# Another order of small products, block products and state steps in the repeated unit of a recurrent-attention and MLP kernel

## The chip, the cores and the metric

The kernel runs on one core of a Trainium2 chip. The metric is device time in microseconds (us) of one execution; times of several executions are given by their median. A profiled execution has a trace besides: a span from its first to its last instruction, and a start and a duration for every instruction.

## The reference

The kernel computes a gated recurrence over 768 steps for 4 batches of 8 heads with 48 channels, and then a normalized MLP on the 384 channels that the heads make together:

```python
for t in range(S):
    state = f[:, :, t, :, None] * state + einsum('bhd,bhde->bhde', k[:, :, t], v[:, :, t])
    y[:, :, t] = einsum('bhd,bhde->bhe', q[:, :, t], state)
x  = y as (B, S, 384)
xn = (x - mean) / sqrt(var + 1e-06) * g_ln
out = x + relu(xn @ w_ch1) @ w_ch2          # w_ch1 384 x 1536, w_ch2 1536 x 384
```

(f is a sigmoid of an input; the einsum of k and v is an outer product. All of it is in float32.)

## The kernel before, in words

**Chunks.** The 768 steps are cut into 12 chunks of 64 steps. A chunk of all four batches has 256 tokens, which lie as two groups of 128 rows. The attention of a chunk and its MLP are written as small stages, and the stages of several chunks run beside each other.

**The order of the work is written by hand.** Two strings of tokens, `START` and `UNIT`, are read by `run` (at the end of the kernel), and each token issues the instructions of one stage. Every engine works off its own instructions in that order, and a wait of one instruction holds all that stand behind it on the same engine. DMAs issued by SP stand in one line too. `START` covers the first chunks. `UNIT` is then run for m = 3 to 11: token `m{m}` is the next step of the MLP of chunk m, `a{n}.x` is stage x of the attention of chunk n = m+1, `a{o}.x` of chunk m+2. `l`/`L` load raw inputs, `p`/`P` split one half of a raw input into two 16-bit planes (a copy on ACT, L439) and send it to DRAM (L440, by POOL for `p`, by SP for `P`), `x` turns it on its way back (a transposing DMA of SP, L454), `s` makes sums for the second MLP layer, `y` sums for the first.

**The attention stages that matter here:**
- `gates` (ACT, L695), `after` and `upto` (DVE scans, L668, L680), `q` (L725 and L728) and `k` (L716) make the scaled q and k, `kept` (L738) the decayed state of the chunk before.
- `carried` (TensorE, L757): 32 small matmuls of the kept state with q. `scores` (L771): 32 small matmuls of k with q. `causal` (DVE, L777) masks them.
- `kt`: a transposing DMA of SP (L454) brings the scaled k back turned. `values` (L807): 32 small matmuls of masked scores with v, and three copies of the result to x on ACT (L816, L818). `chunk` (L845): 32 small matmuls of turned k with v, for chunks up to 10 only. `state` (DVE, L853) adds them to the kept state.
- `stats` (DVE, L830, L831, and two small instructions on POOL, L833, L834), `norm` (DVE, L875) and `turn` (six TensorE transposes, L886, and six ACT copies into `xt`, L888) prepare the MLP.

A small matmul uses a 64 x 64 part of the array, and four parts work side by side; all other matmuls use the array of 128 x 128.

**The MLP of a chunk has 22 steps.** The first layer (`by_blocks`, from L936) is a fast block product: fifteen products of four 128x128x128 matmuls each (L951), whose results stand in PSUM banks with the names bw, bx, by, bv and bz. Behind each product either ACT copies the bank into the block of h that it belongs to (L956), or DVE adds it to the block (L959, L997), and ACT applies the ReLU (L962). `bx` and `by` are used again and again: a product into a bank can only start when the bank's last result has been read. The sums `y` (DVE, L921) are inputs of these products. The second layer is seven products of six matmuls each (L1045), in the order p1, p2, p6, p5, p7, p3, p4; the sums `s` (DVE, L930 to L933) are inputs of p6, p5 and p3. Their results are gathered by DVE (L1053) and POOL (L1053 too): p1x, then p1 += p6, u2x = p1 + x (POOL), p1 += p5, u4x and u4y (POOL), and then u2x, u4y and u4x take p7, p3 and p4 and go out by SP.

**PSUM banks.** Four one-bank tiles go round (`one_bank`, `bufs=4`): the five names of the first layer, the seven products of the second layer and the two transposes of `turn` take them in turn, so each product of the second layer waits until an older result in its bank has been read. The small matmuls have banks of their own; `scores` and `chunk` share one (`shared`).

Of the kernel before, what the change touches and what calls it, by code (L numbers as in the profile page):

```python
# [14 lines left out]
ALU = mybir.AluOpType  # L15
# [300 lines left out]
U m2 m1 p4K0 a5.gates  # L316
"""
UNIT = """
a{o}.after m{m} m{m} a{n}.carried p{o}q1 a{n}.scores a{n}.causal m{m} P{o}q0 m{m} m{m} m{m}
m{m} a{n}.values m{m} p{p}f1 a{o}.upto a{n}.kt m{m} m{m} a{n}.stats m{m} m{m} l{p}k p{p}f0 m{m}  # L320
a{n}.chunk m{m} a{n}.norm m{m} x{o}k x{o}q P{p}k0 m{m} s{m} a{n}.turn a{n}.state l{p}v p{p}k1
m{m} m{m} a{o}.q m{m} a{o}.k L{z}f y{n} p{o}K0 x{p}f l{p}q p{o}K1 m{m} m{m} m{m} a{o}.kept
a{p}.gates
"""


# [1 line left out]
def kernel(  # L328
# [21 lines left out]
    P = 128  # L350
# [585 lines left out]
    def by_blocks(n, h):  # L936


        a, y = y_of.pop(n)
        v, b = late["v"], late["b"]  # L940
        KB = CW // P
        out = {(g, j): h[:, (j - 1) * KB:j * KB, (g - 1) * P:g * P] for g in (1, 2)
               for j in (1, 2, 3)}
        banks = {}

        def product(bank, left, right):
            new = bank not in banks
            if new:
                banks[bank] = one_bank(f"{bank}_{n}").rearrange("p (i t) -> p i t", t=P)
            for i in range(KB):  # L950
                nc.tensor.matmul(banks[bank][:, i], lhsT=right[:, i * P:(i + 1) * P], rhs=left,  # L951
                                 start=new and i == 0, stop=True, skip_group_check=True)
            return banks[bank]

        def copy(to, bank, scale=1.0):
            nc.scalar.activation(out=out[to], in_=bank, func=AF.Copy, scale=scale)  # L956

        def add(to, bank, op=ALU.add):
            nc.vector.tensor_tensor(out=out[to], in0=out[to], in1=bank, op=op)  # L959

        def relu(to, bank=None):
            nc.scalar.activation(out=out[to], in_=out[to] if bank is None else bank, func=AF.Relu)  # L962

        copy((1, 3), product("bw", y[12], b[2, 3]))
        yield
        copy((2, 3), product("bx", y[11], v[11]))
        yield
        copy((1, 1), product("bv", y[3], b[2, 1]))
        yield
        add((1, 3), product("bx", y[9], b[3, 3]))  # L970
        yield
        add((1, 1), product("by", y[4], b[1, 1]))
        yield
        add((1, 1), product("bx", a[1, 3], v[7]), ALU.subtract)
        relu((1, 1))
        yield
        add((1, 3), product("by", a[1, 1], v[13]), ALU.subtract)
        relu((1, 3))
        yield
        copy((1, 2), product("bx", y[10], v[10]))  # L980
        yield
        add((1, 2), product("by", y[1], v[1]), ALU.subtract)
        yield
        copy((2, 2), product("bz", a[2, 2], v[0]), -1.0)
        yield
        add((2, 2), product("bx", y[2], b[3, 2]), ALU.subtract)
        yield
        add((2, 2), product("by", y[14], b[1, 2]))
        relu((2, 2))
        yield  # L990
        add((1, 2), product("bz", y[6], b[2, 2]))
        relu((1, 2))
        yield
        relu((2, 1), product("bx", y[8], v[8]))
        yield
        bank = product("by", y[5], v[5])
        nc.vector.tensor_tensor(out=out[2, 3], in0=bank, in1=out[2, 3], op=ALU.subtract)  # L997
        relu((2, 3))
        yield

    def mlp(n):
# [134 lines left out]
    for m in range(3, NU):  # L1136
# [4 lines left out]
        if m == NU - 2:  # L1141
# [5 lines left out]
                                    op=ALU.min)  # L1147
# [39 lines left out]
```

## Time and profile before

| | |
|---|---|
| median of 3 runs | 437.86 us (437.38 to 440.23) |
| profiled execution | 437.34 us, its span 435.6 us, the rest outside the span 1.7 us |
| granted TensorE clock, mean | 0.985 |
| one repeated unit, from p1 of chunk 6 to p1 of chunk 7 (258.23 to 290.72) and on to p1 of chunk 8 (323.20) | 32.49 and 32.48 us |
| the same from chunk 3 to chunk 4 (160.33 to 193.27) | 32.94 us |
| last matmul ends | 429.2 us |

In the timeline, a row has start, duration, engine, line, operation, output<-inputs, shapes and count; rows of equal instructions that follow each other are merged, and square brackets hold how long the engine had sat idle and what ended that. A matmul in float32 is recorded as two instructions, so a product of four matmuls is x8, a group of 32 small ones x64. PE is TensorE, PEld its weight loads, which run ahead of the matmuls.

### The profile page before, as it was taken

The numbers are of one execution on the slowest core, as the hardware profiler recorded it, in microseconds if no ns is written. First come the engines' busy times: TensorE is split into PE (matmuls) and PEld (weight loads), VectorE is DVE, ScalarE is ACT, GpSimd is POOL, SyncE is SP. The second block draws the span as 40 slices with busy tenths as digits, with TensorE's granted clock in tenths as the row PEclk, the third lists the DMA queues.
The fourth block names the chain that finished last, engine by engine and source line by source line (L and its number), as shares of the span: only waits on it lengthen the run. The fifth ranks groups of instructions, "written<-read, shape, count | busy, mean of one in ns | idle before, by whom it ended". The sixth has DMA issues, their size and how long they took to land.

```text
span 435.6 us, 12925 instructions
## 1 busy us (share of the span) xinstructions
PE 418.5 (96%) x5429; PEld 389.0 (89%) x5429; DVE 338.3 (78%) x539; ACT 214.7 (49%) x364; POOL 125.8 (29%) x148
## 2 busy tenths in 40 slices
PE   5599999999999999999999999999999999999994
PEld 4589987668979999999999999999999999999993
DVE  5998798745986779779779779779779879475451
ACT  2484857443534573574474574574574552350320
POOL 2362453560033026016026016025025015021030
PEclk9699999999999999999999999999999999999998
DMA  9999979887977899699599799699698751401001
GB/s 171 286 212 192 236 227 222 204 198 184 180 154 148 181 208 228 187 200 212 155 211 204 169 187 212 180 188 218 165 196 198 136 117 47 91 2 23 15 9 34
DMA packets 167647, 71.68 MB, mean 165 GB/s; under 512 B 151760, under 2 KB 157840, under 8 KB 167584
## 3 DMA queue, kind: packets, MB, share of 16 engines
q1 hardware_dynamic: 151728, 54.38, 62.9%
q0 software_dynamic: 3872, 12.64, 8.6%
q10 hardware_dynamic: 11984, 3.79, 4.1%
q8 instruction: 44, 0.72, 0.7%
q14 instruction: 19, 0.16, 0.1%
HBM read 28.31 MB, written 23.59 MB: 119 GB/s over the span
## 4 chain that ended last, share of the span: by engine, by line
PE 89%; DVE 3%; ACT 2%; SPq 1%; issue 1%; POOL 1%; DMA 1%; ACTq 0%; DVEq 0%; POOLq 0%
PE pp L1045 31%; PE bx L951 12%; PE by L951 9%; PE ph L1016 7%; PE po L1026 5%; PE bz L951 4%; PE ph L900 3%; PE py L807 3%; PE shared L771 3%; PE py L757 2%; PE bv L951 2%; PE bw L951 2%; PE shared L845 2%; PE xp L886 2%; SPq L474 1%
## 5 line engine op out<-in xcount | busy, mean ns | idle before, releaser
L962 ACT ACTIVATE h<-h 128x512 f32<-128x512 f32 x45 | 28.3, 631 | 49.4 <-DVE h L959 42.0
L1045 PE MATMUL pp<-mixed,h 128*128 128x192 f32 x240 | 42.3, 326 | 0.0
L1045 PE MATMUL pp<-w,h 128*128 128x192 f32 x240 | 42.1, 326 | 0.0
L1045 PE MATMUL pp<-mixed,s 128*128 128x192 f32 x240 | 40.9, 326 | 0.2 <-DVE p1x L1053 0.2
L1045 PEld LDWEIGHTS pp<-mixed,s 128*128 128x128 f32 x240 | 39.2, 190 | 0.5 <-DVE p1x L1053 0.5
L1045 PEld LDWEIGHTS pp<-mixed,h 128*128 128x128 f32 x240 | 39.5, 190 | 0.1
L439 ACT COPY Kplanes<-kh 128x1024 uint16<-128x1024 uint16 x18 | 18.2, 1047 | 42.9 <-DVE kh L716 15.0
L1045 PEld LDWEIGHTS pp<-w,h 128*128 128x128 f32 x240 | 38.7, 190 | 0.3
L668 DVE TENSOR_TENSOR_SCAN after<-gates,ends 128x1040 f32<-128x1040 f32 (+1 forms) x13 | 29.8, 2291 | 6.7 <-ACT gates L699 3.4
L1026 PE MATMUL po<-w,h 128*128 128x384 f32 x96 | 32.3, 489 | 0.0
L1016 PE MATMUL ph<-xt,w 128*128 128x256 f32 x144 | 31.9, 380 | 0.2 <-ACT xt L888 0.2
L959 DVE TENSOR_TENSOR h<-h,by 128x512 f32<-128x512 f32 x36 | 24.8, 688 | 8.6 <-PE by L951 5.0
L1016 PEld LDWEIGHTS ph<-xt,w 128*128 128x128 f32 x144 | 27.1, 190 | 4.3 <-ACT xt L888 0.5
L951 PE MATMUL bx<-y,v 128*128 128x128 f32 x216 | 30.2, 283 | 0.0
L959 DVE TENSOR_TENSOR h<-h,bx 128x512 f32<-128x512 f32 x27 | 18.4, 683 | 13.8 <-PE bx L951 13.8
L680 DVE TENSOR_TENSOR_SCAN upto<-gates,starts 128x1040 f32<-128x1040 f32 (+1 forms) x13 | 28.1, 2158 | 0.5
L1026 PEld LDWEIGHTS po<-w,h 128*128 128x128 f32 x96 | 17.8, 190 | 11.3
L440 POOL DMA_DIRECT2D fhalves<-fplanes x14 | 8.4, 597 | 66.8 <-ACT fplanes L439 66.8
L951 PEld LDWEIGHTS bx<-y,v 128*128 128x128 f32 x216 | 26.2, 191 | 0.9
L1053 POOL TENSOR_TENSOR p1x<-p,x 128x192 f32<-128x192 f32 x10 | 11.6, 1163 | 47.1 <-ACT p L1060 47.1
L562 POOL TENSOR_TENSOR w<-w_0upper,w_0units 128x768 int32<-128x768 int32 x7 | 14.6, 2084 | 28.7 <-DVE w_0upper L560 16.5
L888 ACT ACTIVATE xt<-xp,gain 128x128 f32<-128x128 f32 x72 | 20.0, 380 | 5.4 <-PE xp L886 5.4
(171 smaller groups left out, 961.3 us busy)
## 6 DMA issues: line engine op xcount, KB each, us to landing
w_0words<-in_moe_w_ch_dram SPq DMA_DIRECT2D x7, 768.0 KB, 5.8
v<-in_v_dram SPq DMA_DIRECT2D x46, 96.0 KB, 4.0
Khalves<-Kplanes POOLq DMA_DIRECT2D x16, 256.0 KB, 3.8
kraw<-in_k_dram SPq DMA_DIRECT2D x40, 96.0 KB, 4.4
fhalves<-fplanes POOLq DMA_DIRECT2D x14, 256.0 KB, 4.7
kraw<-in_q_dram SPq DMA_DIRECT2D x36, 96.0 KB, 3.6
fraw<-in_f_logit_dram ACTq DMA_DIRECT2D x27, 96.0 KB, 3.7
khalves<-kplanes POOLq DMA_DIRECT2D x9, 256.0 KB, 3.9
```

The lines of the kernel that those rows point to most:

```text
L439: nc.scalar.copy(out=to, in_=src)
L562: nc.gpsimd.tensor_tensor(out=to.bitcast(I32), in0=upper, in1=units, op=ALU.add)
L668: nc.vector.tensor_tensor_scan(out=at["after"].rearrange(flat)[:, c0:c1][:, ::-1], data0=gt[:, c0 + 1:c1 + 1][:, ::-1], data1=ends.rearran ...
L680: nc.vector.tensor_tensor_scan(out=at["upto"].rearrange(flat)[:, c0:c1], data0=gt[:, c0:c1], data1=starts.rearrange(flat)[:, c0:c1], initi ...
L771: nc.tensor.matmul(ps[half(b), r, e], lhsT=kh[head_rows(r), seg], rhs=qh[head_rows(r), seg], start=True, stop=True)
L888: nc.scalar.mul(out=xt[:, m, g * P:(g + 1) * P], in_=pt[:, m], mul=gain[:, m:m + 1])
L951: nc.tensor.matmul(banks[bank][:, i], lhsT=right[:, i * P:(i + 1) * P], rhs=left, start=new and i == 0, stop=True, skip_group_check=True)
L959: nc.vector.tensor_tensor(out=out[to], in0=out[to], in1=bank, op=op)
L962: nc.scalar.activation(out=out[to], in_=out[to] if bank is None else bank, func=AF.Relu)
L1016: nc.tensor.matmul(ph[:, j], lhsT=w1[:, m, (i + j) * P:(i + j + 1) * P], rhs=xt[:, m], start=m == 0, stop=m == KD - 1)
L1026: nc.tensor.matmul(po, lhsT=h[:, i, g * P:(g + 1) * P], rhs=w2[:, i], start=i == 0, stop=i == KF - 1)
L1045: nc.tensor.matmul(pp, lhsT=a[:, i], rhs=b[:, i], start=i == 0, stop=i == KH - 1)
```

## The change

It does three things, all in the repeated unit; `START` stays as it is.

1. The token string `UNIT` is written anew. `carried` and `scores` stand at the start of the unit, ahead of the first block product. `values` and `chunk` stand next to each other, ahead of the last two block products. `kt` is the first token. `turn` stands between the last two products of the second layer, `stats` behind `chunk`, `norm` and `state` later than before, and the loads and splits are spread otherwise.
2. `by_blocks` runs its fifteen products in another order and with other banks for some.
3. Two helpers, `copied` and `added`, do a product and its reading in one call; the instructions are the same, but for two: block (1, 2) now begins with the copy of one product with scale -1, and the other product is added.

```diff
 UNIT = """
-a{o}.after m{m} m{m} a{n}.carried p{o}q1 a{n}.scores a{n}.causal m{m} P{o}q0 m{m} m{m} m{m}
-m{m} a{n}.values m{m} p{p}f1 a{o}.upto a{n}.kt m{m} m{m} a{n}.stats m{m} m{m} l{p}k p{p}f0 m{m}
-a{n}.chunk m{m} a{n}.norm m{m} x{o}k x{o}q P{p}k0 m{m} s{m} a{n}.turn a{n}.state l{p}v p{p}k1
-m{m} m{m} a{o}.q m{m} a{o}.k L{z}f y{n} p{o}K0 x{p}f l{p}q p{o}K1 m{m} m{m} m{m} a{o}.kept
-a{p}.gates
+a{n}.kt a{n}.carried p{p}f1 a{o}.after a{n}.scores m{m} a{n}.causal m{m} m{m} m{m} P{o}q0 m{m}
+m{m} m{m} m{m} m{m} a{o}.upto m{m} p{o}q1 p{p}f0 m{m} m{m} m{m} x{o}k a{n}.values l{p}k
+a{n}.chunk m{m} a{n}.stats m{m} x{o}q s{m} p{p}k1 P{p}k0 L{z}f a{o}.q a{o}.k m{m} x{p}f m{m}
+m{m} l{p}q l{p}v a{n}.norm m{m} m{m} a{n}.state m{m} p{o}K1 p{o}K0 a{n}.turn a{o}.kept y{n}
+a{p}.gates m{m}
 """
...
+        def copied(to, bank, left, right, scale=1.0):
+            copy(to, product(bank, left, right), scale)
+
+        def added(to, bank, left, right, op=ALU.add):
+            add(to, product(bank, left, right), op)
...
-        copy((1, 3), product("bw", y[12], b[2, 3]))
-        yield
-        copy((2, 3), product("bx", y[11], v[11]))
-        yield
-        copy((1, 1), product("bv", y[3], b[2, 1]))
-        yield
-        add((1, 3), product("bx", y[9], b[3, 3]))
-        yield
-        add((1, 1), product("by", y[4], b[1, 1]))
-        yield
-        add((1, 1), product("bx", a[1, 3], v[7]), ALU.subtract)
...
+        copied((1, 3), "bw", y[12], b[2, 3])
+        yield
+        copied((2, 3), "bx", y[11], v[11])
+        yield
+        copied((1, 1), "by", y[4], b[1, 1])
+        yield
+        added((1, 3), "bx", y[9], b[3, 3])
+        yield
+        added((1, 1), "bv", y[3], b[2, 1])
+        yield
+        added((1, 3), "by", a[1, 1], v[13], ALU.subtract)
+        relu((1, 3))
+        yield
+        added((1, 1), "bx", a[1, 3], v[7], ALU.subtract)
         relu((1, 1))
...
```

(The rest of `by_blocks` is in the same manner: bz, by, bx, bz, by, bx follow, then by with y[5] and bx with y[8] as the last two, the other way round than before.)

**TensorE, end of the first layer of chunk 7.** Before, bz, bx and by are banks of block products, `py` is `values`' output with scores (sc), and `shared<-v,kt` is `chunk`; pp is the first product of the second layer:

```order
L951 MATMUL by_3810<-xt_3590,v_1050 128x128 x4
L807 MATMUL py_3725<-v_3201,sc_3794 64x48 x32
L951 MATMUL bx_3719<-y_3652,v_1048 128x128 x4
L951 MATMUL by_3810<-y_3652,v_1044 128x128 x4
L951 MATMUL bz_3883<-xt_3590,v_1043 128x128 x4
L951 MATMUL bx_3719<-y_3652,w_59 128x128 x4
L951 MATMUL by_3810<-y_3652,w_59 128x128 x4
L951 MATMUL bz_3883<-y_3652,w_59 128x128 x4
L845 MATMUL shared<-v_3201,kt_3876 48x48 x32
L951 MATMUL bx_3719<-y_3652,v_1047 128x128 x4
L951 MATMUL by_3810<-y_3652,v_1045 128x128 x4
L1045 MATMUL pp_8_3979<-w_60,h_3712 128x192 x6
```

And now:

```order
L951 MATMUL bz_3831<-y_3687,w_59 128x128 x4
L951 MATMUL by_3798<-y_3687,w_59 128x128 x4
L951 MATMUL bx_3792<-y_3687,w_59 128x128 x4
L807 MATMUL py_3713<-v_3218,sc_3790 64x48 x32
L845 MATMUL shared<-v_3218,kt_3711 48x48 x32
L951 MATMUL by_3798<-y_3687,v_1045 128x128 x4
L951 MATMUL bx_3792<-y_3687,v_1047 128x128 x4
L1051 MATMUL pp_8_3991<-w_60,h_3783 128x192 x6
```

The two small groups, six block products apart before, now follow each other, and two block products stand behind them. (Lines from L997 on have moved: L1045 is now L1051, L1053 is L1059.)

**TensorE, from the second layer of chunk 7 to the first of chunk 8, with waits.** Shown is the first matmul of each product or group; a name in square brackets is the engine whose work it waits for. The first row is p3, xp are the transposes of `turn`, the next pp is p4, then come `carried` and `scores` and the first block products:

```order
L1051 MATMUL pp_7_3653<-w_60,s_7_3564 128x192 [waits DVE_49]
L886 MATMUL xp_3671<-ident,xn_3628 128x128 [waits DVE_49]
L1051 MATMUL pp_7_3701<-mixed_123,h_3378 128x192 [waits DVE_49]
L757 MATMUL py_3713<-kept_3685,qh_3580 64x48 [waits DVE_49]
L771 MATMUL shared<-qh_3580,kh_3583 64x64 x32
L951 MATMUL bw_3784<-y_3687,w_59 128x128 [waits DVE_49]
L951 MATMUL bx_3792<-y_3687,v_1049 128x128 [waits DVE_49,Activation_49]
L951 MATMUL by_3798<-y_3687,w_59 128x128 [waits DVE_49,Activation_49]
L951 MATMUL bx_3792<-y_3687,w_59 128x128 [waits Activation_49]
```

Before, `turn` stood between p1 and p2, and `carried` and `scores` between bx and bv. Now p4 waits for DVE's reading of p7, whose bank it takes (u4y is the last to read it), and the second bx waits for ACT's copy of the first, with one product between them.

**DVE, beside the second layer of chunk 6.** s are the sums for p6, p5 and p3, p1x and p the gathering of p1, qh and kh the q and k of chunk 8. Before:

```order
L930 TENSOR_TENSOR s_6_3178<-h_2902 128x768
L931 TENSOR_TENSOR s_6_3179<-s_6_3178,h_2902 128x768
L932 TENSOR_TENSOR h_2902<-h_2902 128x6x128
L933 TENSOR_TENSOR s_6_3180<-h_2902,s_6_3179 128x768
L853 TENSOR_TENSOR state<-kept_2895,shared 128x768
L1053 TENSOR_TENSOR p1x_3165<-p1x_3165,pp_6_3209 128x192
L1053 TENSOR_TENSOR p_6_3164<-p_6_3164,pp_6_3219 128x192
L725 TENSOR_TENSOR qh_3228<-turned,upto_2898 128x1024
L728 TENSOR_TENSOR least<-least,total_2899 128x16
L1053 TENSOR_TENSOR p_6_3164<-p_6_3164,pp_6_3231 128x192
L716 TENSOR_TENSOR kh_3241<-qraw,after_2897 128x1024
L921 TENSOR_TENSOR y_3247<-xt_3185 128x256 x2
```

And now:

```order
L933 TENSOR_TENSOR s_6_3159<-h_2973,s_6_3158 128x768
L725 TENSOR_TENSOR qh_3175<-turned,upto_2888 128x1024
L728 TENSOR_TENSOR least<-least,total_2889 128x16
L716 TENSOR_TENSOR kh_3178<-qraw,after_2887 128x1024
L1059 TENSOR_TENSOR p1x_3181<-p1x_3181,pp_6_3195 128x192
L1059 TENSOR_TENSOR p_6_3180<-p_6_3180,pp_6_3205 128x192
L875 TENSOR_SCALAR xn_3223<-x_3096,mv_3143,rstd_3144 128x384 x2
L1059 TENSOR_TENSOR p_6_3180<-p_6_3180,pp_6_3226 128x192
L1059 TENSOR_TENSOR u2x_3182<-u2x_3182,pp_6_3236 128x192
L1059 TENSOR_TENSOR u4y_3184<-u4y_3184,pp_6_3236 128x192
L853 TENSOR_TENSOR state<-kept_2875,shared 128x768
L1059 TENSOR_TENSOR u4x_3183<-u4x_3183,pp_6_3248 128x192
```

qh, least and kh now stand ahead of the gathering of p1, xn stands within it, and state and the sums y come behind it. POOL's u2x, u4x and u4y hang on the rows of p.

More of the change, by code (lines that the diff above doesn't have):

```diff
@@ L962, in relu @@
             nc.scalar.activation(out=out[to], in_=out[to] if bank is None else bank, func=AF.Relu)
-        copy((1, 3), product("bw", y[12], b[2, 3]))
+        def copied(to, bank, left, right, scale=1.0):
[3 more added lines that the diff above has]
+        copied((1, 3), "bw", y[12], b[2, 3])
         yield
-        copy((2, 3), product("bx", y[11], v[11]))
+        copied((2, 3), "bx", y[11], v[11])
         yield
-        copy((1, 1), product("bv", y[3], b[2, 1]))
+        copied((1, 1), "by", y[4], b[1, 1])
         yield
-        add((1, 3), product("bx", y[9], b[3, 3]))
+        added((1, 3), "bx", y[9], b[3, 3])
         yield
-        add((1, 1), product("by", y[4], b[1, 1]))
+        added((1, 1), "bv", y[3], b[2, 1])
         yield
-        add((1, 1), product("bx", a[1, 3], v[7]), ALU.subtract)
+        added((1, 3), "by", a[1, 1], v[13], ALU.subtract)
+        relu((1, 3))
+        yield
+        added((1, 1), "bx", a[1, 3], v[7], ALU.subtract)
         relu((1, 1))
         yield
-        add((1, 3), product("by", a[1, 1], v[13]), ALU.subtract)
-        relu((1, 3))
+        copied((2, 2), "bz", a[2, 2], v[0], -1.0)
         yield
-        copy((1, 2), product("bx", y[10], v[10]))
+        copied((1, 2), "by", y[1], v[1], -1.0)
         yield
-        add((1, 2), product("by", y[1], v[1]), ALU.subtract)
+        added((1, 2), "bx", y[10], v[10])
         yield
-        copy((2, 2), product("bz", a[2, 2], v[0]), -1.0)
-        yield
-        add((2, 2), product("bx", y[2], b[3, 2]), ALU.subtract)
-        yield
-        add((2, 2), product("by", y[14], b[1, 2]))
-        relu((2, 2))
-        yield
-        add((1, 2), product("bz", y[6], b[2, 2]))
+        added((1, 2), "bz", y[6], b[2, 2])
         relu((1, 2))
         yield
-        relu((2, 1), product("bx", y[8], v[8]))
+        added((2, 2), "by", y[14], b[1, 2])
+        yield
+        added((2, 2), "bx", y[2], b[3, 2], ALU.subtract)
+        relu((2, 2))
         yield
@@ L998, in by_blocks @@
         relu((2, 3))
+        yield
+        relu((2, 1), product("bx", y[8], v[8]))
         yield
```

## The prediction, as it was made before the run

> **What bounds the kernel now.** I read the page's busy shares and its chain first, then the busy times by stretch, then the timeline of TensorE through one repeated unit.
>
> ```profile
> PE 418.5 (96%) x5429; PEld 389.0 (89%) x5429; DVE 338.3 (78%) x539; ACT 214.7 (49%) x364; POOL 125.8 (29%) x148
> PE 89%; DVE 3%; ACT 2%; SPq 1%; issue 1%; POOL 1%; DMA 1%; ACTq 0%; DVEq 0%; POOLq 0%
> 160.30:193.30 33.00, 32.81 (x469) 31.81 (x469) 27.94 (x45) 18.14 (x31) 9.57 (x13) 1.00 0.95 206
> 290.72:323.20 32.48, 32.48 (x468) 31.77 (x467) 27.95 (x45) 18.22 (x31) 9.54 (x12) 1.00 0.83 180
> ```
>
> TensorE is busy for 32.48 of the 32.48 us of a unit, at a granted clock of 1.00 (column behind POOL's). No matmul is added or taken away. So a gain can only come from the steps between matmuls: what it costs to go from one group to the next. They are seen in the starts:
>
> ```profile
> 277.44 1.06 PE L951 MATMUL bx<-y,w 128*128 128x128 f32 x8
> 278.33 1.06 PE L951 MATMUL by<-y,w 128*128 128x128 f32 x8
> 279.35 1.16 PE L951 MATMUL bx<-xt,v 128*128 128x128 f32 x8
> 280.34 1.06 PE L951 MATMUL by<-xt,v 128*128 128x128 f32 x8
> 281.33 1.15 PE L807 MATMUL py<-v,sc 64*64 64x48 f32 x64
> 282.41 1.16 PE L951 MATMUL bx<-y,v 128*128 128x128 f32 x8
> 283.40 1.06 PE L951 MATMUL by<-y,v 128*128 128x128 f32 x8
> ...
> 287.96 0.94 PE L845 MATMUL shared<-v,kt 64*48 64x48 f32 x64
> 288.83 1.16 PE L951 MATMUL bx<-y,v 128*128 128x128 f32 x8
> 289.82 1.06 PE L951 MATMUL by<-y,v 128*128 128x128 f32 x8
> 290.72 2.12 PE L1045 MATMUL pp<-w,h 128*128 128x192 f32 x12
> ```
>
> A block product that nothing disturbs takes 0.89 us from start to start (277.44 to 278.33). One ahead of a small group takes 0.99 (280.34 to 281.33), one behind it 0.99 (282.41 to 283.40), and 279.35 starts 1.02 behind its forerunner and takes 0.99 itself, without any small group near. Two kinds of loss, then: switches, and one wait.
>
> **Term 1, two small groups put together.** What does a small group cost when another small one follows, not a big one? `START` has such a pair, `chunk` and then `values`:
>
> ```profile
> 120.04 0.94 PE L845 MATMUL shared<-v,kt 64*48 64x48 f32 x64
> 120.80 1.11 PE L807 MATMUL py<-v,sc 64*64 64x48 f32 x64
> ```
>
> There `chunk` takes 0.76 us, before a big product 0.87 (287.96 to 288.83): leaving costs 0.11. Entering costs 0.99 - 0.89 = 0.10, and the slow first product behind it another 0.10. With `values` and `chunk` side by side one entry, one exit and one slow product go: 0.31 us. It is for the seven units with m = 3 to 9 that have both groups: 7 x 0.31 = 2.2 us. (`carried` and `scores` were a pair already and stay one; the transposes of `turn`, moved from behind p1 to behind p3, are between the same kinds of product as before.) Bounds: nothing, if the pair in the other order pays a switch too, and 2.2; I take 2.2, since the pair in the trace has the same two groups.
>
> The Trainium skill, page TensorEngine Tiling (Array Packing), Key Properties, says that a change of tiling mode drains the array while a move between tiles of one mode doesn't; by that rule the pair pays once, and the trace's 0.76 against 0.87 agrees.
>
> **Term 2, the wait ahead of the third bx.** DVE reads the bank of the second bx late:
>
> ```profile
> 278.61 0.69 DVE L959 TENSOR_TENSOR h<-h,bx 128x512 f32<-128x512 f32 x1 [0.79 <-PE bx L951]
> 279.50 0.69 DVE L959 TENSOR_TENSOR h<-h,by 128x512 f32<-128x512 f32 x1 [0.20 <-PE by L951]
> ```
>
> The read ends at 279.30 and the next product into bx starts at 279.35, 0.05 later. The loss is (1.02 - 0.89) + (0.99 - 0.89) = 0.23 us, in each of nine units: 2.0 us. The cause is that only one product (by) stands between the two bx. In the new order two or three stand between those uses of a bank that DVE reads, so this wait goes.
>
> **Term 3, a new near wait.** The new order has the same pattern once: bx, by, bx at the unit's start, where ACT copies the first bx. In the trace ACT's copy of that product is
>
> ```profile
> 274.53 0.60 ACT L956 ACTIVATE h<-bx 128x512 f32<-128x512 f32 x1 [0.29 <-PE bx L951]
> ```
>
> and the product began at 273.43 (so its copy ends 1.70 after its start; DVE's read in term 2 ended 1.86 after, 279.30 - 277.44). With the 0.05 the bank is free at 1.75. In term 2 it was free at 1.91 and cost 0.23, so nothing is lost up to 1.68. The new one is late by 0.07: 9 x 0.07 = 0.6 us. Bounds: 0 (a copy that begins a little sooner) and 0.2 per unit, as in term 2; I take 0.06, 0.5 in all.
>
> **What moves at no cost, and its cover.** `kt` goes to the head of the unit, in SP's line behind the three result stores and ahead of q's first half; it is needed only by `chunk`, some twelve products later. The sums s must be ready for p6. Before, they began 1.59 after p1 (292.31 against 290.72), held up by the last product of the layer, whose block DVE subtracts. Now that product is the last but one, and `stats` lies ahead of the sums instead. I take 1.3 to 1.6; with 0.99 to the second sum and 0.96 for it, p6's input is ready 3.3 to 3.6 after p1, and p6 is due at 3.9, since the transposes no longer lie between (steps below). If `stats` were later by over 0.3, p6 would wait.
>
> The tightest place is p4. It takes p7's bank, so it waits for u4y on DVE, which waits for POOL's u4y, which waits for u4x, u2x and both additions to p1, which now stand behind qh, least and kh:
>
> ```profile
> 292.31 0.96 DVE L930 TENSOR_TENSOR s<-h 128x768 f32<-128x768 f32 x1 [0.70 <-ACT h L962]
> 293.30 0.96 DVE L931 TENSOR_TENSOR s<-s,h 128x768 f32<-128x768 f32 x1
> 294.18 1.35 DVE L932 TENSOR_TENSOR h<-h 128x768 f32<-128x768 f32 x1
> 295.45 0.94 DVE L933 TENSOR_TENSOR s<-h,s 128x768 f32<-128x768 f32 x1
> 296.31 0.94 DVE L853 TENSOR_TENSOR state<-kept,shared 128x768 f32<-128x768 f32 x1
> 297.18 0.34 DVE L1053 TENSOR_TENSOR p1x<-p1x,pp 128x192 f32<-128x192 f32 x1
> 297.50 0.36 DVE L1053 TENSOR_TENSOR p<-p,pp 128x192 f32<-128x192 f32 x1
> 297.77 1.22 DVE L725 TENSOR_TENSOR qh<-turned,upto 128x1024 f32<-128x1024 f32 x1
> 298.90 0.57 DVE L728 TENSOR_TENSOR least<-least,total 128x16 f32<-128x16 f32 x1
> ```
>
> From the start of the first sum, by the steps of these rows: 0.99, 0.88, 1.27, 0.86 (the four s and h), 1.13 (qh), 0.57, 1.13 (kh, the same shape as qh), 0.32 (p1x), 0.36: 7.5 us. Without POOL at work beside it, h takes 0.9 and not 1.27. So p1 += p6 is done 8.4 to 9.1 after p1's start. Then POOL:
>
> ```profile
> 297.94 1.49 POOL L1053 TENSOR_TENSOR u2x<-p,x 128x192 f32<-128x192 f32 x1 [1.13 <-DVE p L1053]
> 299.90 1.51 POOL L1053 TENSOR_TENSOR u4x<-p,x 128x192 f32<-128x192 f32 x1 [0.47 <-DVE p L1053]
> 301.37 0.78 POOL L1053 TENSOR_TENSOR u4y<-p,x 128x192 f32<-128x192 f32 x1
> 422.23 0.61 POOL L1053 TENSOR_TENSOR u2x<-p,x 128x192 f32<-128x192 f32 x1
> ```
>
> The same addition takes 1.49 under qh and least, and 0.61 where DVE is idle. Chain: u2x 0.61 to 1.49, p1 += p5 0.36, u4x 0.59 to 1.47, u4y 0.6 to 0.78, DVE's u4y 0.35, with five handovers of 0.05: 2.8 to 4.7. p7's bank is free 11.2 to 13.8 after p1.
>
> ```profile
> 292.67 0.82 PE L886 MATMUL xp<-ident,xn 128*128 128x128 f32 x6
> 293.32 2.12 PE L1045 MATMUL pp<-w,h 128*128 128x192 f32 x12
> 295.28 4.06 PE L1045 MATMUL pp<-mixed,s 128*128 128x192 f32 x24
> ```
>
> p4 is due after six products of 1.95 (293.32 to 295.28) and the transposes (0.65): at 12.35. So 1.1 to spare, or 1.5 late. I take spare: in the new order DVE runs only xn and additions that read PSUM while POOL works, and then waits for POOL, as it did around 422.23. Cost 0. `kept`, needed by `carried` one product later, follows p4's release by state, u4x and kept, 0.9 + 0.3 + 0.95, against p4's own 1.95 and the spare.
>
> **The sum.** 437.34 - 2.2 - 2.0 + 0.5 = 433.6 us for the profiled execution; the median of the runs is 0.5 above that execution, so 434.2. The unit becomes 32.48 - 0.31 - 0.23 + 0.06 = 32.0 us. Left as it is: the first unit, which is 0.5 longer than the others (33.00 above), by this wait:
>
> ```profile
> 167.19 2.22 PE L1045 MATMUL pp<-mixed,s 128*128 128x192 f32 x12 [0.19 <-DVE p1x L1053]
> ```
>
> There the old order of `START` meets the new unit; between -0.5 (the wait goes) and +2 (rival B).
>
> **The rivals.**
>
> A, slower: POOL holds p4. Place: p7's bank, units 3 to 10. With 8.4 for the additions and POOL's 1.49, 1.51 and 0.78 it is 0.8 late, 8 x 0.8 = 6.4: 440.0, or 440.6 against the median; with both long ends (1.5 late) 446. It makes the kernel slower from 0.46 late (3.7 / 8). For it: all of u2x and u4x in the steady units are at 1.5. Against it: those lie under qh, least, kh and y, which are no longer beside them. Chance 0.10.
>
> By the Trainium skill's page SBUF — State Buffer, section Who interferes with whom, a DVE instruction with two SBUF inputs and a GpSimd one that reads SBUF lock each other out of a shared port; the trace's 1.49 against 0.61 agrees. By that rule u4x and u4y, beside additions with one PSUM input, go undisturbed, and the chance of A is as low as I set it.
>
> B, a transfer comes late.
>
> ```profile
> qhalves<-qplanes POOLq DMA_DIRECT2D x9, 256.0 KB, 3.0
> turned<-qhalves SPq DMA_TRANSPOSE x9, 6.0
> DMA to landing us min/median/max: 2.3/4.4/8.0
> ```
>
> The splits of q and f share two buffers of planes, so a copy of f on ACT waits for a half of q to land, and the copies of x, `stats` and the sums stand behind it. The last row spans both kinds of q's transfer: a landing 2 us over the median is in it. Lost once, in the first unit, 2 us: 436.2. In every unit it would be more, but there q's half goes out earlier by SP. Chance 0.17.
>
> C, the pair saves nothing, since `chunk` behind `values` pays a switch: 437.34 - 2.0 + 0.5 = 435.8, or 436.4. Against it 120.04. Chance 0.10.
>
> D, more: ACT's copy is in time and the first unit's wait goes as well: 437.34 - 2.2 - 2.0 - 0.5 = 432.6, or 433.2. Chance 0.25.
>
> **How the numbers follow.** My forecast, 434.2, has 0.38. A measurement of this kernel tells about 1% from no change, 4.4 us, so 433.5 is where "faster" begins: D is beyond it and the forecast's lower edge touches it, 0.28. Slower by over 1% (over 442.2) is A with its longer ends, and what I have not thought of: 0.07. The rest is within 1%: 0.65. The range holds D, the forecast, B and C, and leaves out A: 432.4 to 437.4.
>
> **What would show it.** Right: unit 32.0; `values` to `chunk` about 0.97, `chunk` to by 0.87; no step of 1.02 in the block products but one of about 0.95 at the second bx; p4 without idle time before it. Wrong: p4 more than 0.1 late behind the transposes with DVE's u4y as releaser (A), idle time before p6 in the first unit (B), `chunk` behind `values` with a step over 1.05 (C).

## The result, and the profile after

| | before | changed |
|---|---|---|
| median of 20 runs each | 436.84 us (435.14 to 441.3) | 435.19 us (431.99 to 439.96) |
| ratio to the kernel before, 95% interval | | 0.9949 (0.9925 to 0.9973) |
| profiled execution, its span | 437.34, 435.6 us | 436.15, 434.5 us |
| p1 of chunk 3 to p1 of chunk 4 (the first repeated unit) | 32.94 us | 35.99 us |
| an undisturbed unit | 32.48 us | 31.98 us |
| start of the last matmul to the end of the span | 6.7 us | 4.7 us |

The ratio is a gain of 2.2 us (1.2 to 3.3), where 3.7 was forecast. It compares the means of the executions in the faster state of the chip; one of the changed kernel's twenty, the one of 439.96 us, was in the slower state and is left out of it. The busy shares and the chain of the changed kernel's page:

```profile
PE 415.5 (96%) x5429; PEld 387.1 (89%) x5429; DVE 332.9 (77%) x539; ACT 214.6 (49%) x364; POOL 121.8 (28%) x148
PE 80%; DVE 6%; issue 5%; DMA 2%; POOL 2%; SPq 2%; ACT 2%; ACTq 0%; POOLq 0%; DVEq 0%
```

TensorE is busy 3.0 us less for the same matmuls, and yet its last matmul starts later (429.77 against 428.85): in the chain TensorE has 9 points less, and issue (4 points) and DVE (3) have most of them. So it stands idle somewhere. The busy times by stretch say where: one row per unit, from p1 to p1 (stretch and length, then PE, PEld, DVE, ACT and POOL busy, the clock, the DMA share and GB/s).

```profile
160.54:196.53 35.99, 32.49 (x468) 31.44 (x467) 26.91 (x46) 21.86 (x36) 9.04 (x13) 1.00 0.89 198
228.68:260.66 31.98, 31.98 (x468) 31.49 (x467) 27.28 (x46) 18.31 (x30) 9.10 (x12) 1.00 0.81 195
```

The second row is the unit as forecast (32.0). In the first row TensorE is idle for 3.5 us of 35.99.

**The unit, as forecast.** TensorE's timeline at the start of the first layer and at its end:

```profile
246.10 1.06 PE L951 MATMUL bx<-y,v 128*128 128x128 f32 x8
246.99 1.06 PE L951 MATMUL by<-y,w 128*128 128x128 f32 x8
247.89 1.12 PE L951 MATMUL bx<-y,w 128*128 128x128 f32 x8
248.84 1.06 PE L951 MATMUL bv<-y,w 128*128 128x128 f32 x8
...
256.97 1.15 PE L807 MATMUL py<-v,sc 64*64 64x48 f32 x64
257.94 0.90 PE L845 MATMUL shared<-v,kt 64*48 64x48 f32 x64
258.77 1.16 PE L951 MATMUL by<-y,v 128*128 128x128 f32 x8
259.77 1.06 PE L951 MATMUL bx<-y,v 128*128 128x128 f32 x8
260.66 1.63 PE L1051 MATMUL pp<-w,h 128*128 128x192 f32 x9
```

`values` to `chunk` takes 0.97, `chunk` to `by` 0.83, `by` to `bx` 1.00 and `bx` to p1 0.89: one entry, one exit, one slow first product. The second `bx` takes 0.95 to its successor (247.89 to 248.84), the only block product away from small groups that isn't at 0.89.

**The first repeated unit.** TensorE, and then POOL, SP and ACT around it; the last fence has the landing of POOL's transfer (us from its issue):

```profile
160.54 1.47 PE L1051 MATMUL pp<-w,h 128*128 128x192 f32 x8
163.13 2.87 PE L1051 MATMUL pp<-w,h 128*128 128x192 f32 x16 [1.12 <-ACT h L962]
168.38 4.14 PE L1051 MATMUL pp<-mixed,s 128*128 128x192 f32 x24 [2.38 <-DVE s L931]
```

```profile
155.21 0.54 POOL L440 DMA_DIRECT2D qhalves<-qplanes  x1 [10.40 <-ACT qplanes L439]
```

```profile
154.15 0.53 SPq L440 DMA_DIRECT2D qhalves<-qplanes  x1
```

```profile
153.88 1.04 ACT L439 COPY qplanes<-kraw 128x1024 uint16<-128x1024 uint16 x1
161.50 1.04 ACT L439 COPY fplanes<-fraw 128x1024 uint16<-128x1024 uint16 x1 [6.58 <-DMA qhalves<-qplanes]
162.45 1.14 ACT L962 ACTIVATE h<-h 128x512 f32<-128x512 f32 x2
163.50 0.46 ACT L816 COPY x<-py 128x384 f32<-128x384 f32 x1
```

```profile
qhalves<-qplanes POOLq DMA_DIRECT2D x1, 256.0 KB, 6.2
```

Read these rows from the last fence up. The half of q that POOL sent at 155.21 landed 6.2 later, at 161.4. The copy of f's second half on ACT started at 161.50, behind 6.58 us of idle time. Behind it stand two ReLUs, for which p1 waited 1.12 us, and the copies of x, behind these on DVE the statistics and the sums, for which p6 waited 2.38 us. This is rival B's place.

By its waits, the copy of f takes over the buffer of POOL's half of q in this unit, and in the others that of SP's half. SP sends its half at 154.15 here, 6.4 ahead of p1, and 9.6 ahead in a later unit (283.3 against 292.93). There the copy of f follows the copy of q without a wait.

**The pair of profiles, in sum.** Last matmul to last matmul: start of the first unit's p1 +0.2, first unit +3.05, the five full units behind it -2.0 (they would be -2.5, but for stops that are told below), the two short ones -0.3: +0.9. Behind the last matmul -2.0. Together the -1.1 of the spans.

### The profile page after: what moved, and what is told of

Its sections match the earlier page's. It is cut to its first block, busy times and chain, and to the rows that moved or that the text cites. A ratio compares the mean times of both kernels' runs of the same rounds, so it can differ in the third digit from the quotient of the medians.

```text
span 434.5 us, 12953 instructions
## 1 busy us (share of the span) xinstructions
PE 415.5 (96%) x5429; PEld 387.1 (89%) x5429; DVE 332.9 (77%) x539; ACT 214.6 (49%) x364; POOL 121.8 (28%) x148
## 4 chain that ended last, share of the span: by engine, by line
PE 80%; DVE 6%; issue 5%; DMA 2%; POOL 2%; SPq 2%; ACT 2%; ACTq 0%; POOLq 0%; DVEq 0%
PE pp L1051 27%; PE bx L951 10%; PE by L951 9%; PE ph L1022 7%; PE ph L900 4%; PE po L1032 4%; PE bz L951 3%; PE shared L771 2%; PE py L757 2%; PE py L807 2%; PE bw L951 2%; PE bv L951 2%; PE xp L886 2%; PE shared L845 2%; DMA qhalves<-qplanes 1%
## 5 line engine op out<-in xcount | busy, mean ns | idle before, releaser
L1051 PE MATMUL pp<-mixed,s 128*128 128x192 f32 x240 | 40.7, 326 | 2.4 <-DVE s L931 2.4
L1051 PE MATMUL pp<-mixed,h 128*128 128x192 f32 x240 | 42.4, 326 | 0.0
L1051 PE MATMUL pp<-w,h 128*128 128x192 f32 x240 | 41.1, 327 | 1.1 <-ACT h L962 1.1
L1051 PEld LDWEIGHTS pp<-mixed,s 128*128 128x128 f32 x240 | 39.2, 190 | 2.6 <-issue 2.6
L1051 PEld LDWEIGHTS pp<-w,h 128*128 128x128 f32 x240 | 38.9, 190 | 1.7 <-ACT h L962 1.4
L1051 PEld LDWEIGHTS pp<-mixed,h 128*128 128x128 f32 x240 | 39.1, 190 | 0.1
L959 DVE TENSOR_TENSOR h<-h,bx 128x512 f32<-128x512 f32 x36 | 24.6, 683 | 17.1 <-PE bx L951 16.4
L440 POOL DMA_DIRECT2D qhalves<-qplanes x9 | 4.9, 545 | 96.5 <-ACT qplanes L439 96.5
L951 PE MATMUL bx<-y,v 128*128 128x128 f32 x216 | 28.7, 275 | 0.0
L833 POOL TENSOR_SCALAR rstd<-mv 128x2 f32<-128x2 f32 (+1 forms) x13 | 8.1, 626 | 62.2 <-DVE mv L831 61.9
L439 ACT COPY fplanes<-fraw 128x1024 uint16<-128x1024 uint16 x18 | 18.9, 1054 | 8.9 <-DMA qhalves<-qplanes 6.6
L439 ACT COPY kplanes<-kraw 128x1024 uint16<-128x1024 uint16 x18 | 18.2, 1044 | 9.1 <-DMA kraw<-in_k_dram 4.4
```

The lines of the kernel that those rows point to most:

```text
L439: nc.scalar.copy(out=to, in_=src)
L1051: nc.tensor.matmul(pp, lhsT=a[:, i], rhs=b[:, i], start=i == 0, stop=i == KH - 1)
```

## The experiments

My theory: the unit's gain is that of the three terms, and the first unit gives part of it back, since ACT waits there for a transfer. The rivals: the first unit is behind for another reason, whatever the buffer; or the gain comes from one part of the change alone, and the other does nothing.

**Three buffers of planes.** The edit:

```diff
-        planes = raws.tile([P, 2, 64 * H], U16, tag="planes", name=f"{name}planes{n}_{i}")
+        planes = raws.tile([P, 2, 64 * H], U16, tag="planes", bufs=3, name=f"{name}planes{n}_{i}")
```

> The changed kernel with three buffers of planes instead of two; nothing else. Theory (the first repeated unit loses its 4.0 us because the copy of f's second half on ACT waits for the landing of a half of q whose buffer it takes over, and the ReLUs, the copies of x, the statistics and the sums stand behind that copy): the copy of f goes right behind the copy of q, no idle time before the fourth matmul of p1, p6 in time; first unit 36.0 -> 32.0 to 33.0 us (up to 1 may stay, since q itself still lands late and its scaling stands ahead of the gathering of p1 that p4 waits for), other units 32.0, whole time 2 to 4 us below the changed kernel's profiled 436.15 and 1 to 3 below its median, so a ratio of 0.989 to 0.993 to the kernel before. Rival 1 (the sums come late because START hands the first unit over with DVE and SP behind, whatever the buffer): first unit stays at 35 to 36 us. Rival 2 (the loss is the transfer's own slowness and moves on to the scaled q): first unit 34 to 35 us with the idle time before p4 instead of p6.

Median 432.37 us, ratio 0.9862 (0.9825 to 0.9898). The first unit by stretch, and ACT in it:

```profile
164.91:196.89 31.98, 31.98 (x469) 31.49 (x467) 26.88 (x46) 18.41 (x30) 8.71 (x12) 1.00 0.83 195
```

```profile
158.25 1.04 ACT L439 COPY qplanes<-kraw 128x1024 uint16<-128x1024 uint16 x1
159.18 1.05 ACT L439 COPY fplanes<-fraw 128x1024 uint16<-128x1024 uint16 x1
```

The copy of f follows the copy of q at once, and the first unit takes 31.98 us, like any other. In all other profiles of the new token string and products with three buffers (below) it is as long as the units behind it too: 31.98, 31.92, 31.92 and 32.24. The buffer is the cause; both rivals fall. (The execution that was profiled was the longest of its six, 438.02, and 4.4 of that lie ahead of the first unit, 164.91 against 160.54; its units are read, not its length.) The ratio is better than expected; more on that below.

**The same third buffer in the kernel before** (the same edit there).

> The kernel before with three buffers of planes instead of two. In the kernel before no copy on ACT waited for a landing of planes in the repeated units, so theory 1 (the third buffer helps only where the changed order hands q's buffer to f) expects 0 to -1 us: units of 32.48, the first 33.0 or 0.5 less, ratio 0.997 to 1.001. Rival (the third buffer also shortens START, or all units, in both kernels, and so is a gain of its own): 1.5 us or more, ratio below 0.996.

Median 437.71, ratio 1.0004 (0.9973 to 1.0035), first unit 32.93, units 32.48 (one of 33.60 has a stop that is told below). The third buffer is worth nothing by itself. What it repairs is made by the new order.

**The changed kernel again**, beside others on one chip, unchanged.

> The changed kernel once more, on the chip and beside the runs of the other three. Theory (the first unit loses what the copy of f waits for, and that is a landing which differs from run to run): units of 32.0, first unit = 32.0 + 3.0 us + (start of the copy of f's second half - start of p1), between 32.5 and 36.5; ratio 0.993 to 0.998. Rival (a fixed loss): first unit 36.0 again.

Ratio 0.9941 (0.9912 to 0.997), first unit 33.22. ACT's copy of f, and the stretch:

```profile
159.07 1.04 ACT L439 COPY fplanes<-fraw 128x1024 uint16<-128x1024 uint16 x1 [3.81 <-DMA qhalves<-qplanes]
```

```profile
160.89:194.11 33.22, 32.22 (x469) 31.47 (x467) 27.18 (x46) 20.05 (x34) 9.16 (x13) 1.00 0.80 196
```

The copy started 1.82 ahead of p1, for which the theory's sum gives 33.2. Four executions with two buffers can be put in a row (loss is the first unit less an undisturbed unit of the same kernel):

| kernel | copy of f, start less p1's start | loss | loss less copy |
|---|---|---|---|
| changed | 161.50 - 160.54 = +0.96 | 35.99 - 31.98 = 4.01 | 3.05 |
| changed, again | 159.07 - 160.89 = -1.82 | 33.22 - 31.98 = 1.24 | 3.06 |
| groups apart (below) | 158.53 - 160.27 = -1.74 | 33.63 - 32.32 = 1.31 | 3.05 |
| old products (below) | 160.52 - 160.98 = -0.46 | 36.34 - 33.67 = 2.67 | 3.13 |

Each us of the landing is a us of the unit, from 3.05 ahead of p1 on. It is no accident of one execution either: POOL issues 5.3 ahead of p1, and with the median landing of this kind of transfer (3.7 in the changed kernel's trace) the copy starts 1.6 ahead, which is about 1.4 us lost.

**q's second half split earlier.**

```diff
-m{m} m{m} m{m} m{m} a{o}.upto m{m} p{o}q1 p{p}f0 m{m} m{m} m{m} x{o}k a{n}.values l{p}k
+m{m} p{o}q1 m{m} m{m} m{m} a{o}.upto m{m} p{p}f0 m{m} m{m} m{m} x{o}k a{n}.values l{p}k
```

> The changed kernel with two planes buffers, but the split of q's second half two products earlier (behind the fifth block product instead of the ninth). Theory (late landing of that half): it is issued 3 to 4.5 us sooner in the first unit, lands before the copy of f needs the buffer, first unit at 32.0 to 33.0 us; in the other units the copy of q stands on ACT ahead of two bank copies and can cost 0 to 0.2 us of a unit (32.0 to 32.2). Whole time about 1 to 3 us below the changed kernel. Rival 1 (the start of the unit is behind for another reason): first unit stays at 35 to 36.

(In the strings this split goes from behind the tenth product to behind the sixth: four products, not two. The half was issued 7.3 ahead of p1 instead of 5.3.) Median 436.16, ratio 0.995 (0.9915 to 0.9985): nothing won against the changed kernel. The first unit's copy of f came at 156.92, 3.9 ahead of p1, and there was no wait for the sums; its 33.61 us hold one stop of TensorE of 1.5 us (below). But in the unit behind it the copy of f now waited 3.87 us for q, in the unit of chunk 8 p6 waited 0.7 us for the sums, and one block product of each full unit took 0.98 instead of 0.89 (units of 32.1 to 32.2 where little else happens), which a bank that ACT reads late would explain. The remedy moved the wait from one unit to others, which bears out what waits, and is no remedy.

**The two small groups apart.**

```diff
-a{n}.chunk m{m} a{n}.stats m{m} x{o}q s{m} p{p}k1 P{p}k0 L{z}f a{o}.q a{o}.k m{m} x{p}f m{m}
+m{m} a{n}.chunk a{n}.stats m{m} x{o}q s{m} p{p}k1 P{p}k0 L{z}f a{o}.q a{o}.k m{m} x{p}f m{m}
```

> The changed kernel with chunk one block product behind values instead of right behind it; everything else as it is. Theory (a small group next to another saves one entry, one exit and one slow first product, 0.31 us): seven units 32.0 -> 32.3 us, 2.2 us in all; chunk's last step 0.87, a block product between the two groups 0.99. Rival (order of the two groups makes no difference, the gain of the unit comes from the block products alone): units stay at 32.0 us.

TensorE in an undisturbed unit:

```profile
254.52 1.15 PE L807 MATMUL py<-v,sc 64*64 64x48 f32 x64
255.60 1.16 PE L951 MATMUL by<-y,v 128*128 128x128 f32 x8
256.69 0.94 PE L845 MATMUL shared<-v,kt 64*48 64x48 f32 x64
257.56 1.16 PE L951 MATMUL bx<-y,v 128*128 128x128 f32 x8
258.55 1.63 PE L1051 MATMUL pp<-w,h 128*128 128x192 f32 x9
```

The full units behind the first take 32.32 us, 0.34 more than with the two groups side by side: term 1 was 0.31. From `values` to p1 it is 4.03 us here and 3.69 in the changed kernel (256.97 to 260.66). Ratio 0.999 (0.9938 to 1.0043).

**The old products in the new token string** (the old body of `by_blocks`, all else changed).

> The new token string with the old order of block products. Theory (the wait ahead of the third bx is made by one product's distance between two uses of a bank that DVE reads, and the new order of products takes it away): the wait of 0.1 to 0.15 us and the slow product behind it come back, and more of them, since values no longer stands among those products: units of 32.2 to 32.5 us against 32.0. Rival (the small groups at the start of the unit have taken the wait away, not the order of products): units stay at 32.0 us. The first unit's loss is independent of the products and stays between 1 and 4 us.

Median 449.09, ratio 1.0234 (1.0192 to 1.0277): 33.67 us a unit, far above what either theory gave. The wait ahead of the third `bx` is back, as expected (a step of 0.23 where 0.11 is normal, 0.10 for the slow product behind it, and 0.05 once more with its 0.10): 0.37. The other 1.3 were not expected. A unit, what TensorE waited for in it, and DVE behind its p1 at 231.18:

```profile
231.18:264.85 33.67, 32.59 (x469) 31.61 (x467) 26.90 (x45) 18.45 (x31) 7.71 (x12) 1.00 0.83 185
```

```profile
PE pp L1045 <- DVE s L931: 1.1, 1, 1.1
```

```profile
231.52 0.56 DVE L830 BATCH_NORM_STATS2 stats<-x 128x6 f32<-128x384 f32 x1 [2.03 <-ACT x L818]
...
234.22 0.96 DVE L930 TENSOR_TENSOR s<-h 128x768 f32<-128x768 f32 x1 [0.69 <-ACT h L962]
```

The statistics stand ahead of the last subtraction on DVE and wait for the copies of x on ACT, which wait behind two ReLUs; the sums begin 3.0 behind p1 instead of 1.3, and p6 is 1.24 late (5.14 behind p1 instead of 3.90).

**The last two products alone, back in the old order**, with three buffers of planes:

```diff
-        bank = product("by", y[5], v[5])
-        nc.vector.tensor_tensor(out=out[2, 3], in0=bank, in1=out[2, 3], op=ALU.subtract)
-        relu((2, 3))
-        yield
         relu((2, 1), product("bx", y[8], v[8]))
         yield
+        bank = product("by", y[5], v[5])
+        nc.vector.tensor_tensor(out=out[2, 3], in0=bank, in1=out[2, 3], op=ALU.subtract)
+        relu((2, 3))
+        yield
```

> The changed kernel with three buffers of planes, and the last two block products of a unit back in the old order (the one that ACT reads alone first, the one that DVE subtracts last). Theory (the 1.4 us that p6 waited in the kernel with all the old products is made by this pair alone: the subtraction stands on DVE behind the statistics, which wait for the copies of x, and the sums stand behind it): p6 waits 1.2 to 1.5 us in each of the units 3 to 9, units of 33.2 to 33.5 instead of 31.98, 9 to 10 us in all. Rival (the wait came from the delays of the old products before, 0.3 us of them, or from the copy of f): no more than 0.3 us before p6, units of 31.98 to 32.3.

Ratio 0.9962 (0.9927 to 0.9997), units of 32.24. My theory falls, the rival stands: p6 is late by 0.18 (4.08 behind p1), not by 1.2. In the two shorter units at the end neither is right: they take 31.79 and 30.10 instead of 31.26 and 28.09, since p6 is 0.45 and 1.04 late there and a `bx` waits 0.8 for DVE in the last one. DVE behind p1 at 225.49:

```profile
224.76 0.56 DVE L830 BATCH_NORM_STATS2 stats<-x 128x6 f32<-128x384 f32 x1 [2.03 <-ACT x L818]
...
227.47 0.96 DVE L930 TENSOR_TENSOR s<-h 128x768 f32<-128x768 f32 x1 [0.69 <-ACT h L962]
```

The statistics wait here too, but start 0.73 ahead of p1, not 0.34 behind it. So the 1.24 us of the kernel above have two parts: this order of the last two, and 1.07 us by which the copies of x came later there. In that kernel three additions stand on DVE behind the scan `upto`, the last of them for a block whose ReLU stands on ACT ahead of the copies of x (DVE from 225.19 to 229.49, ACT's two ReLUs at 228.92); that this is what moved the copies I read from the trace, and did not try alone.

**The old token string with the new products.**

> The old token string with the new order of block products. Theory (half of the unit's gain is two small groups side by side, the other half the products' order): the products alone take away the wait ahead of the third bx, but the two groups stay apart; the scan on DVE stands just ahead of the last additions, so the last but one product waits about 0.4 us for its bank: units of 32.2 without and 32.7 us with that wait. Rival (the products' order alone brings the whole gain): 32.0 us. No copy waits for a half of q here, so the first unit is within 0.6 us of the others.

Median 439.37, ratio 1.0048 (1.0023 to 1.0073): slower than before. The unit:

```profile
226.60:259.50 32.90, 32.58 (x468) 31.77 (x467) 28.02 (x47) 18.32 (x30) 9.30 (x12) 1.00 0.89 191
```

```profile
257.62 1.16 PE L951 MATMUL by<-y,v 128*128 128x128 f32 x8 [0.32 <-DVE h L959]
```

The expected wait behind `chunk` costs 0.39, and another wait, at the `by` before it, 0.25 (a step of 0.26 and the slow product behind it), which was not expected. One full unit, the one from p1 of chunk 8, has neither wait and takes 32.26, the 32.2 of the theory. The first unit is 32.94. So each half of the change alone makes the kernel slower, the products by 0.4 us a unit and the tokens by 1.2; together they make it 0.5 faster.

**bx ahead of bw, and three buffers.**

```diff
-        copied((1, 3), "bw", y[12], b[2, 3])
-        yield
         copied((2, 3), "bx", y[11], v[11])
         yield
+        copied((1, 3), "bw", y[12], b[2, 3])
+        yield
```

> The changed kernel with three buffers of planes, and with the first two block products in the other order (the bx product with v11 first, then bw), so that two products and not one lie between the two early uses of bx. Theory (the 0.06 us ahead of the second bx is ACT's copy of that bank, one product away): the step of 170 ns at the second bx goes back to 112, units 31.98 -> 31.92 us, 0.5 us in all, first unit 32 to 33; ratio to the kernel before 0.985 to 0.991. Rival (the first product of a unit is held by another bank or another reader, since the banks go round): the step moves elsewhere and units stay at 31.98 or get longer.

Median 432.83, ratio 0.9887 (0.985 to 0.9923). TensorE at the second bx, and a unit:

```profile
244.16 1.06 PE L951 MATMUL bx<-y,w 128*128 128x128 f32 x8
245.06 1.06 PE L951 MATMUL bv<-y,w 128*128 128x128 f32 x8
```

```profile
256.88:288.80 31.92, 31.92 (x468) 31.43 (x467) 27.27 (x46) 18.21 (x30) 9.10 (x12) 1.00 0.85 196
```

The second `bx` takes 0.90, not 0.95, and the unit is 0.06 shorter: term 3, to the hundredth. The last unit gives it back (28.52 against 28.09), since there the first `bx` waits 0.3 us for its sum y. In time the two kernels with three buffers are not told apart.

**Where TensorE stops for nothing.** In several profiles it stood still, mostly in the middle of a product or a small group, with "issue" as releaser. The rows below are of three buffers alone, and then of three buffers with two warming matmuls more at the very start (`d d` became `d d d d`):

> The changed kernel with three buffers of planes and two more warming matmuls (four instructions of TensorE) at its very start, where it waits for its first loads. In the runs so far TensorE stood still now and then in the middle of a product, waiting for nothing, at its instructions 4802, 5313, 7618 and 8129 or 8130: all 193 or 194 over a multiple of 256. Theory (it waits there for the next 256 instructions, which come by DMA): such stops, if any, stand again 190 to 195 over a multiple of 256, but four instructions earlier in the work. Rival (they belong to the work, a weight or a bank): they stand at the same matmul of the same product, 197 or 198 over. The time: units of 31.98, first unit 32 to 33, ratio 0.985 to 0.991 to the kernel before, as with three buffers alone.

```profile
214.31 0.61 PE L951 MATMUL bx<-y,v 128*128 128x128 f32 x4
215.49 0.60 PE L951 MATMUL bx<-y,v 128*128 128x128 f32 x4 [0.57 <-issue]
```

```profile
306.04 0.61 PE L951 MATMUL bx<-y,v 128*128 128x128 f32 x4
306.87 0.60 PE L951 MATMUL bx<-y,v 128*128 128x128 f32 x4 [0.22 <-issue]
```

Counted over TensorE's records in order (matmuls and weight loads together), from 0, a stop falls on these numbers. What it cost is the product or group that holds it less the same one undisturbed:

| kernel | records of the stops (lost, us) | the count modulo 256 |
|---|---|---|
| changed | 5313 (0.2), 7617 (0.3) | 193 each |
| changed, again | 5313 (0.5) | 193 |
| three buffers | 5313 (0.7), 7617 (0.8), 8129 (0.4) | 193 each |
| q earlier | 4801 (1.5), 7617 (0.7) | 193 each |
| old products | 5313 (0.2), 8129 (0.6) | 193 each |
| bx ahead of bw, both times | 5313 (0.4), 5313 (0.3) | 193 each |
| last two products | 5313 (0.2) | 193 |
| old tokens; before with three buffers | 8129 (0.2); 8129 (1.1) | 193 each |
| two warming matmuls more | 5313 (0.7), 8129 (0.4) | 193 each |

The added matmuls moved the work by eight records (four instructions' worth were expected; each matmul in float32 leaves four records), and the stops stayed at the same numbers: at 5313 the record is now the first of its product and not one in the middle. So they belong to the place in the instruction stream and not to the work, as the theory said. In all these traces the page has the row "q8 instruction: 44, 0.72": 44 transfers of 16 KB, for some 10,940 records of TensorE, one for each 249.

The traces also hold the start and the end of each of these transfers. Numbered from 0, transfer k - 1 goes with record 256k + 193. In all 17 stops of the table TensorE went on 1.25 to 1.81 us behind the end of that transfer, and at the 543 other such records of the 14 traces (k from 2 to 41) it was never less than 1.24 us behind it. So the stops are waits for the next block of instructions. Why that block is late at just these four records, and only in some executions, is open.

The median, 433.33, ratio 0.9896 (0.9863 to 0.9929), is a second measurement of three buffers.

**The end of the program, twice.** Nothing is edited; the kernel before and the one with bx ahead of bw, profiled again.

> The kernel before, profiled again. From the start of the last matmul to the end of the span it took 6.7 us in its first profile, 6.2 and 5.9 in the two other kernels with the old token string, and 4.7 in seven of the eight executions with the new one (6.4 in the other); the chain there is the landing of the last result. Theory 1 (it goes with the kernel): 5.9 to 6.8 us again. Theory 2 (it goes with the execution): 4.7 us as likely as not. The units stay at 32.48 us, the first at 32.9.

> The changed kernel with three buffers of planes and bx ahead of bw, profiled again. Theory 1 (the time behind the last matmul goes with the kernel): 6.2 to 6.6 us again, as in its first profile. Theory 2 (it goes with the execution): 4.7 us as likely as not, as in the other kernels with the new token string. Units of 31.92 us, the first one too, the stops of TensorE at other positions than in its first profile or at the same one, 193 over a multiple of 256.

6.0 us and 4.7 us. The second kernel had 6.4 before, so the time behind the last matmul isn't fixed by the kernel. Yet it was 5.9 to 6.7 in all four profiles with the old token string and 4.7 in nine of the ten with the new one. The issues of the last result stand 0.7 us behind the start of the last matmul in both. In the two profiles of the second kernel it is the landing of ACT's half of that result that differs (us from its issue, first profile and second):

```profile
out_dram<-u2x ACTq DMA_DIRECT2D x1, 48.0 KB, 3.9
out_dram<-u2x ACTq DMA_DIRECT2D x1, 48.0 KB, 2.2
```

In the profiles with the old token string this landing isn't recorded; SP's half, where it is, landed 1.9 us after its issue, as in the others. So there a late landing of ACT's half is likely but not shown, and why it is late more often with the old string is left open.

## Why the prediction was right, and where it was short

**Term 1** (two small groups put together, 0.31 a unit) was right: 0.34 when they are parted again. The bound "nothing" (rival C) is out. By the Trainium skill's page TensorEngine Tiling (Array Packing), Key Properties, only a change of tiling mode drains the array; the trace agrees: `values` to `chunk` takes 0.97 and `chunk` to `by` 0.83, where parted groups take 1.08 and 0.87.

**Terms 2 and 3** (the wait ahead of the third bx goes, 0.23; a near wait comes, 0.06) were right. 32.48 - 0.34 - 0.23 + 0.06 is 31.97, and 31.98 was measured; with the first two products exchanged the 0.06 goes as well. Term 3 was 0.06 a unit in the trace, the size that was taken from inside its bounds, and its working fits: the weight load of the second `bx` starts at 247.84, 0.05 behind the end of ACT's copy (247.19 + 0.60), while undisturbed loads start 0.11 ahead of their product, here at 247.78.

**The sums** were to be ready 3.3 to 3.6 behind p1, with p6 due at 3.9. DVE's and TensorE's rows in the unit that starts at 260.66:

```profile
261.92 0.93 DVE L930 TENSOR_TENSOR s<-h 128x768 f32<-128x768 f32 x1
262.88 0.96 DVE L931 TENSOR_TENSOR s<-s,h 128x768 f32<-128x768 f32 x1
```

```profile
264.56 4.06 PE L1051 MATMUL pp<-mixed,s 128*128 128x192 f32 x24
```

They begin 1.26 behind p1 and are ready at 3.18; p6 starts at 3.90. The cover named, the order of the last two products, is worth 0.26 a full unit when taken away, and 2.5 us in the two shorter units together.

**Rival A** (POOL holds p4) fell as argued. POOL, DVE and TensorE in that unit:

```profile
270.65 0.59 POOL L1059 TENSOR_TENSOR u4x<-p,x 128x192 f32<-128x192 f32 x1 [0.56 <-DVE p L1059]
271.20 0.59 POOL L1059 TENSOR_TENSOR u4y<-p,x 128x192 f32<-128x192 f32 x1
```

```profile
271.82 0.35 DVE L1059 TENSOR_TENSOR u4y<-u4y,pp 128x192 f32<-128x192 f32 x1 [0.86 <-POOL u4y L1059]
```

```profile
273.02 2.12 PE L1051 MATMUL pp<-mixed,h 128*128 128x192 f32 x12
```

The bank is free at 272.17, 11.5 behind p1 (11.2 to 13.8 was the range), and p4 starts at 12.36 without idle time. u4x and u4y take 0.59 each, where u4x took 1.5 under kh and u4y 0.78 under the sums y. By the Trainium skill's page SBUF — State Buffer, section Who interferes with whom, a DVE instruction with at most one SBUF input, outside its two-port modes, does not contend with GpSimd. The trace agrees as far as it goes: DVE's addition to u2x, with one input in PSUM, runs beside the first 0.3 us of u4x, and for the rest of the two DVE waits for POOL.

**The step that failed** is "Left as it is: the first unit". Its place and mechanism were named in rival B, with a chance of 0.17 and 2 us for a landing out of the ordinary. The unit loses 1.4 us with the median landing already, and 1.2 to 4.0 in four executions. I had the row for the landing, but not the time at which the copy of f is due: 3.05 ahead of p1, one us for one us behind it, while POOL's issue stands 5.3 ahead. The prediction does say that SP's half of q goes out earlier in the other units; it does not say that in the first unit the copy of f takes over the buffer of POOL's half. Its bounds for the first unit, -0.5 and +2, held in the second profile of the changed kernel (33.22 against 32.94, +0.28) and not in the first (+3.05).

**The sum.** By matmuls, three buffers bring -4.3 us: -0.5 up to p1 of chunk 3 (20.25 against 20.75, from the start of the matmuls ahead of it that write `po`, the second layer of an earlier chunk; they start at 140.29 in the changed kernel and at 139.58 before), -1.0 in the first unit, -2.5 in the five units behind it, -0.3 in the two short ones. The first unit's own wait in the kernel before, 0.46, is in it (the extra of rival D); without it, it is -3.8, against the forecast's -3.7. Two buffers give back 1.2 to 4.0 of that in the traces. By time, two buffers have -2.2 and -2.6 us and three have -6.0, -4.5 and -4.9, so 2 to 4 us lie between them. The intervals of the three measurements end at -4.5, -3.1 and -3.4: the -4.3 lies within two of the three. What came on top may be the landing at the end; that is argued, not shown.

**Luck.** The measured 435.19 is 1.0 from the forecast 434.2, but the level was off as well: the three runs shown had a median of 437.86, twenty have 436.84. This 1.0 hides half of what was missing: between the medians the gain is 1.65, 2.0 less than 3.7. What held is the unit and its three terms; that the range held too is owed to rivals B and C, which it was made to include.

## What to carry to other kernels

When an order by hand is written for the repeated unit, go through its first pass by itself: the queues come in from another order, buffers may be handed out otherwise there, and one late landing on an engine that works in order is paid, once the slack is used up, by all that stands behind it. For each wait on a transfer, work out when its result is due and compare that with the issue and the median landing, and not only with the worst. And parts of an order are judged together: here each half alone made the kernel slower, by 0.4 and 1.2 us a unit, and both made it 0.5 faster.

## What the runs showed of the hardware

TensorE, busy without a gap, stopped now and then for 0.2 to 1.5 us with no other engine to wait for, always 193 records over a multiple of 256, and not in every execution. Each time it went on 1.25 to 1.81 us behind the end of a 16 KB transfer of the instruction queue: it had waited for the next block of its own instructions. By the Trainium skill's page Runtime: NRT & Kernel Launch, section Instruction fetch mechanics, instructions come in blocks of 256 by DMA, and crossing a block costs little that is seen; the place agrees with these runs, and the cost here is up to 1.5 us, in a program whose DMA engines are busy for 0.8 to 0.9 of the units that hold a stop. Up to three such stops were seen in one execution; they may be part of why the runs of the changed kernel spread over 8 us.
